# First pair's score operands padded with zeros, its first shift after four blocks, and every queue's order chosen with a backward pass

## The chip, the cores and the metric

One core of one Trainium2 chip runs the whole program. The metric is the device time of one execution in microseconds (us); of several runs the median counts. Five queues work side by side: TensorE (PE, matmuls, with PEld for its weight loads), VectorE (DVE), ScalarE (ACT), GpSimd (POOL) and SyncE (SP), which issues every DMA here. The operands lie in a memory of 128 partitions (SBUF); matmuls write into the banks of PSUM.

## The reference, cut to what matters

Attention with averaged query pairs is followed by a gated unit. For 8 batches and 8 heads, keys 1152 x 64 and 576 averaged queries:

```python
q_pool = q.reshape(B, H, S // 2, 2, D).mean(axis=3)        # 576 x 64
scores = q_pool @ k.T / sqrt(D)                            # 576 x 1152
scores = scores - scores.max(-1)
attn = exp(scores); attn = attn / (attn.sum(-1) + 1e-9)
x = attn @ v                                               # heads side by side: 8 x 576 x 512
h = relu(x @ w_in); u, v = h[..., :512], h[..., 512:]
v_n = (v - mean(v)) / sqrt(var(v) + 1e-6)
out = (u * (w_spatial @ v_n + b_spatial)) @ w_out
```

Everything is float32 outside. Inside, a number is split into a float16 head and a float16 rest, so that a product takes two or three float16 matmuls.

## The kernel before, in words

The 64 heads are worked in 32 pairs of two heads, four pairs to a batch. Each pair goes through these generators:

- `prep(i)` loads q and k, adds the two queries of each average (POOL), squares and sums q and k (ACT), makes power-of-two scales from that (one small matmul, then three DVE operations), and splits q and k: heads by ACT (`head`), rests by DVE (`rest`) or, from pair 8 on and in pairs 0 and 1, by POOL (`tensor_sub`). In pairs 2 to 7 (`i < EARLY`) DVE makes the rests of k. Each head has 64 rows, so a pair's two heads lie in the lower and upper 64 partitions; DMAs copy rows into operands of 128 rows (`khi`, `qhi`: k's head twice, q's head and rest below each other) and of 66 rows (`klo`, `xq`: k's rest against q's head, plus two rows that carry the shift).
- `maxima(i)` makes 27 matmuls of 128 queries by 384 keys (9 blocks t, 3 key parts n), each followed by a maximum on DVE (L751). Blocks 0 to 3 belong to the first head, block 4 holds the tails of both heads, blocks 5 to 8 belong to the second.
- `shift` turns the maxima of some blocks into two float16 rows (DVE L764 to L769, a PE transposition L773, DVE L775) and DMAs them into rows 64 and 65 of `xq` (L778). Before, the first shift covers blocks 0 to 4, the second 5 to 8.
- `attention(i)` makes 18 main score tiles (two matmuls each, L950 and L951), an exponential of each on ACT (L956), for most a split into head and rest on POOL (L976), and the products with v (PE L846 to L864), plus four tail tiles (L963, L967, ACT L972).
- From pair 8 on, `gated_unit` works on two finished batches in between: L1036 and L1103 (w_in), L1147 (spatial), L1190 (w_out). The weights arrive as float64 and are made float32 by DVE and ACT in `from_double` on tiles of 128 x 1024; `in_weights` is stepped through from pair 0 on.

The order on each queue is not the order of this program text. The class `Order` records all instructions, gives each a cost, and `pin` plays them forward on a model: of the instructions that are ready on a queue it takes the one that stands first in the text, and then ties each instruction to the one before it on its queue. `SLACK` delays a successor on another engine, `in_turn` keeps ACT's first instructions in text order.

In pairs 0 and 1 (`DIRECT`) the maxima of the first head read `xq` and `kn` in place, on 64 rows; those of the second head need the DMA copies `qhi` and `khi`.

## Time and profile before

| what | before |
|---|---|
| median of 3 runs | 1167.14 us (1166.41, 1167.14, 1171.51) |
| the profiled execution's own time | 1172.69 us |
| its span, first to last instruction | 1170.9 us |
| PE busy | 1139.1 us (97%) |
| DVE, ACT, POOL busy | 858.7, 891.6, 846.5 us |
| first maximum's matmul starts | 10.72 us |
| first exponential of scores starts | 27.35 us |
| first gated-unit matmul (L1036) starts | 256.31 us |
| mean granted TensorE clock | 0.992 |

The profiled execution was 5.55 us slower than the median run, and 1.79 us of its time lie outside its span. How to read it: PE is the engine with the least idle time, so time is lost where PE is idle or its granted clock is low. A busy PE is not always a PE at its peak, since ends of matmuls are modelled; the spacing of matmul starts is the better measure. Idle time of the other engines costs nothing by itself.

### The profile page before, as it was taken

To read this page: it belongs to the slowest core of one execution; us is meant where nothing else is said; L and a number is where in the kernel's file an instruction comes from. 1 tells how busy PE (TensorE), PEld (TensorE's weight loads), DVE (VectorE), ACT (ScalarE), POOL (GpSimd) and SP (SyncE) were. 2 spreads that over 40 slices of the span, in tenths; PEclk is the share of its full clock that TensorE was granted. 3 is DMA by queue.
4 is the path that set the end of the run, shared out by engine and by line. 5 is a ranking of instruction groups with operands and counts; after the bars stand their busy time and mean duration, and the time that the engine had idled before them with its cause. 6 is when DMAs were issued, how large, how long until landed. Compare 5 with 4: busy or idle time off the path is not lost.

```text
span 1170.9 us, 33542 instructions
## 1 busy us (share of the span) xinstructions
PE 1139.1 (97%) x13297; PEld 723.9 (62%) x13297; DVE 858.7 (73%) x2240; ACT 891.6 (76%) x1697; POOL 846.5 (72%) x732
## 2 busy tenths in 40 slices
PE   4999999999999999999999999999999999999998
PEld 1567777776566666666666666666666666665453
DVE  5699999867899878766678668866668777832644
ACT  6698789988787978788777977978777877754423
POOL 3566566778887988889787978898788877883000
PEclk9799999999999999999999999999999999999999
DMA  6575456444432443565323454265433431121002
GB/s 217 153 210 147 111 164 205 139 118 139 125 107 73 122 144 103 140 180 143 90 71 85 139 133 122 69 168 163 115 104 82 127 88 20 38 65 37 1 1 81
DMA packets 88990, 132.97 MB, mean 114 GB/s; under 512 B 39872, under 2 KB 48064, under 8 KB 88832
## 3 DMA queue, kind: packets, MB, share of 16 engines
q1 hardware_dynamic: 88832, 130.82, 39.8%
q8 instruction: 104, 1.70, 0.6%
q14 instruction: 54, 0.44, 0.1%
HBM read 81.20 MB, written 9.44 MB: 77 GB/s over the span
## 4 chain that ended last, share of the span: by engine, by line
PE 82%; DVE 7%; DMA 4%; ACT 3%; POOL 1%; issue 1%; SPq 1%; DVEq 0%; ACTq 0%; POOLq 0%
PE pss L950 9%; PE pss L951 9%; PE pm L745 8%; PE pw L1190 7%; PE pw L1147 7%; PE pw L1103 6%; PE pw L1036 6%; PE o L853 5%; PE o L864 5%; PE o L859 5%; DVE mt L751 3%; PE o L846 2%; PE pss L1036 1%; PE pss L1147 1%; DMA kt<-in_kT_dram 1%; PE pss L1190 1%
## 5 line engine op out<-in xcount | busy, mean ns | idle before, releaser
L976 POOL TENSOR_TENSOR pt<-pt 128x512 f16<-128x512 f32 x528 | 580.9, 1115 | 173.2 <-ACT pt L956 167.8
L956 ACT ACTIVATE pt<-pss,esc 128x512 f32<-128x512 f32 x576 | 389.2, 690 | 115.4 <-PE pss L951 107.9
L751 DVE TENSOR_REDUCE mt<-pm 128x1 f32<-128x384 f32 x733 | 387.5, 549 | 106.3 <-PE pm L745 90.6
L950 PE MATMUL pss<-qhi,khi 128*128 128x512 f16 x576 | 220.6, 383 | 3.9 <-ACT ptl L972 2.1
L951 PE MATMUL pss<-xq,klo 66*128 66x512 f16 x576 | 221.1, 384 | 0.0
L745 PE MATMUL pm<-khi,qhi 128*128 128x384 f16 x643 | 198.1, 326 | 5.2 <-DMA khi<-kn 3.4
L853 PEld LDWEIGHTS <-pt 128*128 128x128 bf16 x2112 | 125.1, 99 | 68.4 <-issue 3.0
L853 PE MATMUL o<-vp,pt 128*128 128x65 f16 x2112 | 157.3, 193 | 1.5 <-DVE xm L872 1.5
L864 PE MATMUL o<-vp,pt 128*128 128x65 f16 x2112 | 154.7, 193 | 0.0
L859 PE MATMUL o<-vp,pt 128*128 128x64 f16 x2112 | 153.1, 193 | 1.1 <-DVE vp L405 1.1
L864 PEld LDWEIGHTS <-pt 128*128 128x128 f16 x2112 | 113.7, 98 | 36.6 <-issue 1.8
L859 PEld LDWEIGHTS <-pt 128*128 128x128 bf16 x2112 | 101.8, 98 | 3.8 <-issue 1.2
L745 PEld LDWEIGHTS <-qhi 128*128 128x128 f16 x744 | 71.1, 99 | 45.6 <-issue 7.1
L1036 PE MATMUL pw<-wi_h,xg 128*128 128x512 f16 x240 | 89.2, 378 | 0.0
L1103 PE MATMUL pw<-xg,wi_h 128*128 128x512 f16 (+1 forms) x336 | 82.6, 325 | 0.0
L751 DVE TENSOR_REDUCE mt<-pw 128x1 f32<-128x384 f32 x131 | 70.4, 546 | 16.5 <-PE pw L745 11.6
L976 POOL TENSOR_TENSOR ptl<-ptl 128x1152 f16<-128x1152 f32 x32 | 69.9, 2184 | 17.4 <-ACT ptl L972 17.4
L972 ACT ACTIVATE ptl<-pss,esc 128x256 f32<-128x256 f32 (+1 forms) x128 | 64.1, 500 | 23.7 <-PE pss L967 23.7
L1147 PE MATMUL pw<-ws_h,vv 128*128 128x512 f16 x216 | 79.2, 379 | 0.0
L1190 PE MATMUL pw<-wo_h,vv 128*128 128x512 f16 x216 | 78.5, 378 | 0.0
L951 PEld LDWEIGHTS <-klo 66*128 66x128 f16 x576 | 56.4, 98 | 31.1 <-issue 8.6
L950 PEld LDWEIGHTS <-khi 128*128 128x128 f16 x576 | 56.5, 98 | 21.3 <-issue 4.3
(255 smaller groups left out, 2503.8 us busy)
## 6 DMA issues: line engine op xcount, KB each, us to landing
vt<-in_v_dram SPq DMA_DIRECT2D x56, 576.0 KB
qt<-in_qT_dram SPq DMA_DIRECT2D x32, 576.0 KB
kt<-in_kT_dram SPq DMA_DIRECT2D x32, 576.0 KB
khi<-kn SPq DMA_DIRECT2D x128, 144.0 KB
out_dram<-row SPq DMA_DIRECT2D x24, 256.0 KB
qhi<-xq SPq DMA_DIRECT2D x64, 72.0 KB
klo<-klo SPq DMA_DIRECT2D x32, 144.0 KB
u<-in_w_in_dram SPq DMA_DIRECT2D x3, 1024.0 KB
```

The lines of the kernel that those rows point to most:

```text
L745: nc.tensor.matmul(pm[:, :W], lhsT=q[:, c0 : c0 + P], rhs=k[:, n * NB : (n + 1) * NB, :], start=True, stop=True,)
L751: nc.vector.reduce_max(out=mt[:, t, n : n + 1], in_=pm[:, :W], axis=AX.X)
L853: nc.tensor.matmul(o[:, t], lhsT=top[:, cols], rhs=vp[:, D : D + D1], start=c == 0 and t == 0, stop=False, skip_group_check=True,)
L859: nc.tensor.matmul(o[:, t, 0:D], lhsT=top[:, cols], rhs=vp[:, 0:D], start=False, stop=False, skip_group_check=True)
L864: nc.tensor.matmul(o[:, t], lhsT=rst[:, cols], rhs=vp[:, D : D + D1], start=False, stop=c == NC - 1, skip_group_check=True,)
L950: nc.tensor.matmul(o, lhsT=khh[:, h, c, :], rhs=qhl[:, h, q], start=True, stop=False)
L951: nc.tensor.matmul(o, lhsT=KL[0:KR, h, c, :], rhs=X[0:KR, h, q], start=False, stop=True)
L956: nc.scalar.activation(pt, ps, AF.Exp, bias=0.0, scale=esc)
L976: nc.gpsimd.tensor_sub(t.bitcast(F16)[..., 0::2], t, t.bitcast(BF16)[..., 1::2])
L1036: nc.tensor.matmul(ph, lhsT=rows(xa, cc, c0, c0 + P), rhs=wa[:, cc, DH:DF], start=n == 0, stop=n == 3 * NCC - 1,)
L1147: nc.tensor.matmul(pv, lhsT=l, rhs=r[:, 0:MAIN], **fl)
L1190: nc.tensor.matmul(py, lhsT=ga[:, fc, c0 : c0 + P], rhs=wa[:, fc, :], start=m == 0, stop=m == end - 1)
```

## The change

- **First pair's operands.** For pair 0, q's heads go into `xz`, a tile of 128 rows per head whose other 64 rows are zero; the maxima of both heads multiply it with `kn`, which holds both heads' keys, so no row copy comes before them. The score products of pair 0 run on all 128 rows of `klo` and `xq` (rows 66 to 127 zero), and the copy of the two constant rows (L678 before) is gone for pair 0. New memsets on DVE zero these rows. The first half of k's head is made by DVE, not ACT.
- **First shift.** In pair 0 it covers blocks 0 to 3 (`cut = 4`), and pair 0's tail tiles come after main tiles 5 to 8 rather than 1 to 4.
- **Smaller moves.** `lnp` is made by POOL, not DVE. For batch 0 the squares of v take one ACT instruction of 1152 columns per pair, not two of 576. In pairs 4 to 7 the rests of k move from DVE to POOL, with one more ACT pass over k. `in_weights` is stepped from pair 4 on (`W_PAIR`), at rate 0.4 instead of 0.14.
- **Order.** `SLACK` has new values. `pin` runs twice: a forward pass, a backward pass over the same model (which gives each instruction the latest time at which it may start), and a second forward pass that takes, of the ready instructions, the most urgent. The forward pass also models a slower TensorE clock after idle windows. `in_turn` keeps DVE's first instructions in text order as well.

```diff
-    SLACK = {("Pool", "PE"): 1400, ("Activation", "PE"): 300, ("DVE", "PE"): 400, ("SP", "PE"): 1000}
+    SLACK = {("Pool", "PE"): 724, ("Activation", "PE"): 435, ("DVE", "PE"): 444, ("SP", "PE"): 1510, ("PE", "DVE"): 50}
+    WINDOW, COLD, WARM = 3413.3, 0.34, 0.765
+    PASSES = 2
...
-                    n = min(n for n in ns if at[n] <= t)
+                    n = min((n for n in ns if at[n] <= t), key=rank.__getitem__)
...
+            if e == "PE":
+                columns, weight = g.stream[n]
+                u = t
+                while True:
+                    while u >= until:
+                        share, work = work / self.WINDOW, 0.0
+                        rate = (2.4 if share > self.WARM else 1.2) if rate < 2 else (1.2 if share < self.COLD else 2.4)
+                        until += self.WINDOW
...
+    def backward(self, g, begin, own):
...
+                    t = max(free[e], min(due[n] - own[n] for n in ns))
+                    if best is None or t < best[0]:
+                        n = max((n for n in ns if due[n] - own[n] <= t), key=begin.__getitem__)
...
+        rank = range(len(prog))
+        for k in range(self.PASSES):
+            if k:
+                rank = self.backward(g, begin, own)
+            turns, begin, own, span = self.forward(g, rank)
...
-    for t in klo:
+    for t in klo[1:]:
         nc.gpsimd.memset(t[D:KR, 1], -MROW)
+    nc.vector.memset(klo[0][D:P], 0.0)
+    nc.vector.memset(klo[0][D:KR], -MROW)
+    nc.vector.memset(xq[0][D:P], 0.0)
+    for h in range(2):
+        nc.vector.memset(qhi[NSET - 1][(1 - h) * D : (2 - h) * D, h], 0.0)
...
+        if i == 0:
+            xz, kl = qhi[NSET - 1], khi[NSET - 1][:, 0]
+            kn = ld.tile([P, NC, P], F16, name="kn")
+            nc.vector.tensor_scalar_mul(kn[:, 0:5], k0[:, 0:5], s_k)
+            head(xz[lower, 0], q0[lower], s_q[lower])
+            head(kn[:, 5:NC], k0[:, 5:NC], s_k)
+            head(xz[upper, 1], q0[upper], s_q[upper])
...
+            for a, z in ((0, 5), (5, NC)):
+                nc.scalar.activation(k0[:, a:z], k0[:, a:z], AF.Copy, bias=0.0, scale=s_k)
+                nc.gpsimd.tensor_sub(kl[:, a:z], k0[:, a:z], kn[:, a:z])
+            nc.sync.dma_start(out=KL[lower, 0], in_=kl[lower])
+            factors(st, s, r)
+            load_kq(1)
+            yield
+            rest(qhl[lower, 1], q0[lower], s_q[lower], xz[lower, 0])
+            rest(qhl[upper, 1], q0[upper], s_q[upper], xz[upper, 1])
+            nc.sync.dma_start(out=qhl[upper, 0], in_=qhl[lower, 1])
...
-            if i < EARLY:
+            if i < 4:
                 head(kn[:, a:z], k0[:, a:z], s_k)
                 yield
                 rest(KL[:, 0, a:z], k0[:, a:z], s_k, kn[:, a:z])
...
-                    if i < DIRECT and h == 0:
+                    if i == 0:
+                        q, k = st["xz"][:, h], st["kn"]
+                    elif i == 1 and h == 0:
...
-            if t == 4:
-                yield from shift(st, mt, pm, 0, 5)
+            if t == cut - 1:
+                yield from shift(st, mt, pm, 0, cut)
...
+        rows = P if i == 0 else KR
...
-            Pace(weights, W_RATE, W_AT if i == 0 else 0),
+            Pace(weights if i >= W_PAIR else None, W_RATE),
```

On PE, pair 0, behind the twelve maxima of blocks 0 to 3 (`xq`, `qhi` and `qd` hold q, `kn`, `khi` and `klo` hold k). Before:

```order
L745 MATMUL pm<-kn,xq_113 128x384
...
L950 MATMUL pss<-qhi_119,khi_116 128x512
...
L732 MATMUL pw<-kn,qd_122 128x384
...
L773 MATMUL pw<-ident_h,wide_133 128x128
...
L745 MATMUL pm<-khi_116,qhi_119 128x384
...
L951 MATMUL pss<-xq_113,klo_107 128x512
```

and now:

```order
L861 MATMUL pm<-kn,qhi_123 128x384
...
L846 MATMUL pw<-kn,qd_124 128x384
...
L889 MATMUL pm<-ident_h,wide_137 128x128
...
L861 MATMUL pw<-kn,qhi_123 128x384
...
L1068 MATMUL pss<-qhi_121,khi_118 128x512
L1069 LDWEIGHTS klo_107
L1069 MATMUL pss<-xq_114,klo_107 128x512
```

The transposition of the first shift (L773, now L889) no longer stands behind all three tail maxima, the second head's maxima read `kn` and not the copy `khi`, and between the transposition and the first complete score product stand the third tail maximum and ten maxima of the second head, where nine of the second head stood before.

On SP, the DMAs of pair 0 from the load of pair 1's keys on. Before:

```order
L546 DMA kt<-in_kT_dram 128x1152
L673 DMA klo_107<-klo_107 64x1152
L674 DMA qhi_119<-xq_113 64x576
L675 DMA xq_113<-xq_113 64x576
L676 DMA khi_116<-kn 64x1152
L677 DMA khi_116<-kn 64x1152
L678 DMA klo_107<-klo_107 2x1152
L778 DMA xq_113<-mr 1x5x128 x2
```

and now:

```order
L629 DMA kt<-in_kT_dram 128x1152
L894 DMA xq_114<-mr 1x4x128 x2
L767 DMA qhi_121<-qhi_121 64x576
L769 DMA xq_114<-qhi_123 64x576
L770 DMA qhi_121<-qhi_123 64x576
L771 DMA khi_118<-kn 64x1152
```

The shift rows (`mr`) now go out right behind the load, ahead of the second head's copies.

On DVE, the second shift of the second pair, with a step of the weights' conversion (`vv`, 128 x 1024). Before:

```order
L764 TENSOR_REDUCE pw<-mt 128x4
L751 TENSOR_REDUCE mt<-pw 128x1
L765 TENSOR_SCALAR pw<-pw,lnp 128x4
L432 SCALAR_TENSOR_TENSOR vv<-vv 128x1024
L768 CAST wide_134<-pw 128x4
L751 TENSOR_REDUCE mt<-pm 128x1
L769 TENSOR_TENSOR wide_134<-pw,wide_134 128x4
```

and now:

```order
L880 TENSOR_REDUCE pw<-mt 128x4
L942 RECIPROCAL den<-den 128x4
L881 TENSOR_SCALAR pw<-pw,lnp 128x4
L941 TENSOR_SCALAR dent<-pm 128x1
...
L884 CAST wide_138<-pw 128x4
L867 TENSOR_REDUCE mt<-pm 128x1
L1044 TENSOR_SCALAR xt<-pm,dent 64x64 x2
L885 TENSOR_TENSOR wide_138<-pw,wide_138 128x4
```

The conversion of the weights has left this place: its first step on DVE now comes among the maxima of the third pair. Small operations of the values (`den`, `dent`, `xt`) stand there instead.

More of the change, by code (lines that the diff above doesn't have):

```diff
@@ L3 @@
 from contextlib import ExitStack
+from types import SimpleNamespace
 import concourse.bass as bass
@@ L165, in cost @@
         if lane == "SP":
-            if "DMA" not in ins.opcode:
+            if "DMA" not in ins.opcode and "Dma" not in ins.opcode:
                 return 0, 2400
@@ new lines, in streamed, with forward @@
+    def streamed(self, ins):
+        x = ins.ins[0].bass_ap
+        wide = x.dtype == F32
+        return math.prod([d[1] for d in x.ap][1:]) * (4 if wide else 1), x.ap[0][1] / 128 * (0.5 if wide else 1)
+    def forward(self, g, rank):
+        lane, cost, shared = g.lane, g.cost, g.shared
+        size = len(lane)
+        left = [len(pre) + len(beg) for pre, beg in zip(g.before, g.begun)]
+        ready = {e: [n for n in range(size) if lane[n] == e and not left[n]] for e in self.LANES}
+        due, there, begin, own = ([0.0] * size for _ in range(4))
+        free = dict.fromkeys(self.LANES, 0.0)
+        held, dve, wire = (0.0, 0.0), 0.0, 0.0
+        until, work, rate = self.WINDOW, 0.0, 1.2
+        turns = []
+        for _ in range(size):
@@ L263, in pin @@
                 dve = t + out - 139
+            if e == "PE":
[6 more added lines that the diff above has]
+                        until += self.WINDOW
+                    z = u + columns / rate
+                    if z <= until:
+                        work += (z - u) * weight
+                        break
+                    columns -= (until - u) * rate
+                    work += (until - u) * weight
+                    u = until
+                out += max(0, z - t - long)
+                long = max(long, z - t)
             if e == "SP":
-                wire = max(wire, t + own) + 0.58 * (out - 2400)
+                wire = max(wire, t + long) + 0.58 * (out - 2400)
                 end = wire + 1700 + 0.42 * (out - 2400)
@@ L268, in pin @@
                 end = t + out
-            free[e] = t + own
-            if e in last:
-                tc.add_manual_dep(prog[n], last[e], dep, reason="order")
-            last[e] = prog[n].name
-            for m, through in after[n]:
+            begin[n], own[n] = t, long
+            free[e] = t + long
+            for m, through in g.after[n]:
                 left[m] -= 1
@@ L284, in pin @@
                     ready[lane[m]].append(m)
-        self.span = max(free.values())
+        return turns, begin, own, max(free.values())
+    def backward(self, g, begin, own):
+        lane, cost = g.lane, g.cost
+        size = len(lane)
+        left = [len(after) for after in g.after]
+        ready = {e: [n for n in range(size) if lane[n] == e and not left[n]] for e in self.LANES}
+        due, done = [0.0] * size, [0.0] * size
+        free = dict.fromkeys(self.LANES, 0.0)
+        for _ in range(size):
+            best = None
+            for e, ns in ready.items():
+                if ns:
+                    t = max(free[e], min(due[n] - own[n] for n in ns))
+                    if best is None or t < best[0]:
+                        n = max((n for n in ns if due[n] - own[n] <= t), key=begin.__getitem__)
+                        best = (t, e, n)
+            _, e, n = best
+            ready[e].remove(n)
+            done[n] = free[e] = max(free[e] + own[n], due[n])
+            for pre, through in ((g.before[n], True), (g.begun[n], False)):
+                for m in pre:
+                    x = done[n]
+                    if through and lane[m] != e:
+                        x += cost[m][1] + self.DELAY.get((lane[m], e), 52)
+                    elif through and e != "PE":
+                        x += cost[m][1] + 34
+                    due[m] = max(due[m], x)
+                    left[m] -= 1
+                    if not left[m]:
+                        ready[lane[m]].append(m)
+        return [-t for t in done]
@@ L723, in maxima @@
         mt = sm.tile([P, NT, 3], F32, name="mt", bufs=2)
+        cut = 5 if i else 4
         for t in range(NT):
@@ L1259, in attn_sgu_kernel @@
         next(n)
-    drain(prep(0))
-    order.in_turn(tc)
+    load_kq(1, True)
+    ready = prep(0)
+    for _ in range(5):
+        next(ready)
+    order.in_turn(tc, "Activation")
     first = maxima(0)
-    for _ in range(18):
+    for _ in range(13):
         next(first)
+    order.in_turn(tc, "DVE")
+    for _ in range(2):
+        next(first)
+    drain(ready)
     for n in norms:
```

195 lines of the change are left out of this document (108 added, 87 removed).

## The prediction

> **What bounds the kernel now.** I read the page's busy times first, then the busy times by stretch, then the timeline of the first 70 us and the groups of DVE. The page says that PE has little idle time, and its row of the granted clock that the second of forty slices is slow:
>
> ```profile
> PE 1139.1 (97%) x13297; PEld 723.9 (62%) x13297; DVE 858.7 (73%) x2240; ACT 891.6 (76%) x1697; POOL 846.5 (72%) x732
> PEclk9799999999999999999999999999999999999999
> ```
>
> The stretches say where the rest goes (columns: stretch, its length, then busy time of PE, PEld, DVE, ACT and POOL, granted clock, DMA share, GB/s):
>
> ```profile
> 0.00:20.00 20.00, 7.40 (x23) 2.34 (x23) 11.81 (x30) 13.22 (x28) 10.40 (x20) 1.00 0.80 265
> 20.00:40.00 20.00, 15.09 (x107) 7.07 (x107) 13.71 (x35) 15.06 (x29) 9.96 (x9) 0.84 0.39 87
> 34.00:51.00 17.00, 17.00 (x81) 7.45 (x81) 8.73 (x17) 8.10 (x14) 9.85 (x9) 0.51 0.76 203
> 51.00:61.00 10.00, 10.00 (x146) 8.36 (x145) 7.62 (x23) 9.60 (x20) 4.72 (x5) 1.00 0.31 108
> 60.00:256.00 196.00, 188.13 (x2364) 140.34 (x2363) 178.73 (x457) 171.56 (x333) 132.28 (x107) 1.00 0.55 158
> 256.00:420.00 164.00, 161.41 (x1938) 101.20 (x1937) 140.44 (x352) 141.24 (x278) 140.84 (x117) 1.00 0.43 120
> 420.00:1060.00 640.00, 639.88 (x7997) 407.01 (x7995) 451.28 (x1218) 495.79 (x932) 537.14 (x468) 1.00 0.39 107
> ```
>
> From 420 to 1060 us PE is idle for 0.12 us in 640: nothing is to be had there, and what is won earlier stays won, because PE then does the same matmuls at the same pace. PE is idle for 12.6 us in the first 20 and for 4.9 in the next 20. From 34 to 51 it is never idle, but at a granted clock of 0.51. From 60 to 256 (pairs 1 to 7) it is idle for 7.9 us, with DVE busy for 91% and ACT for 88%: three engines close to full. From 256 to 420 it is idle for 2.6 us.
>
> The start in detail:
>
> ```profile
> 9.00 0.15 DVE L389 TENSOR_SCALAR qks<-pm 128x2 int32<-128x2 int32 x1
> 9.18 0.77 ACT L402 ACTIVATE xq<-qt,qks 128x576 f16<-128x576 f32 x1 [0.71 <-DVE qks L389]
> 10.72 0.48 PE L745 MATMUL pw<-kn,xq 64*128 64x384 f16 x1 [2.04 <-ACT kn L402]
> 13.43 0.55 DVE L751 TENSOR_REDUCE mt<-pw 128x1 f32<-128x384 f32 x1
> 13.89 0.55 DVE L751 TENSOR_REDUCE mt<-pm 128x1 f32<-128x384 f32 x1
> 19.07 0.18 DVE L764 TENSOR_REDUCE pw<-mt 128x5 f32<-128x15 f32 x1
> 20.37 0.28 DVE L775 CAST mr<-pw 10x128 f16<-10x128 f32 x1 [0.39 <-PE pm L378]
> 22.86 1.51 SPq L778 DMA_DIRECT2D xq<-mr  x2
> 23.75 0.48 PE L745 MATMUL pm<-khi,qhi 128*128 128x384 f16 x1 [3.42 <-DMA khi<-kn]
> 26.93 0.60 PE L951 MATMUL pss<-xq,klo 66*128 66x512 f16 x2
> 27.35 1.26 ACT L956 ACTIVATE pt<-pss,esc 128x512 f32<-128x512 f32 x2 [1.07 <-PE pss L951]
> ```
>
> DVE's maxima come every 0.46 us and set the pace from 11 to 19. Then PE waits 3.42 us for a row copy of k, and the shift rows, ready at 20.65 (20.37 + 0.28), leave only at 22.86, because SP waits for another copy, the constant rows of `klo`:
>
> ```profile
> SPq L678 <- DMA klo<-klo: 3.2, 1, 3.2
> ```
>
> **Term A, the first pair's start: -2.3 us.** Until the scales (9.15) nothing changes: ACT's squares set that time. The new memsets on DVE are of 1152, 576, 2304 and twice 288 columns; by 1.07 us for 1152 columns on POOL (3.21 for three, below) they take 4.3 us, from about 1 to 5.3, and the slow copies behind them (2.10 in the row below, and a cast of at most that) end between 7.4 and 9.5. The scales are done at 9.15 now, so they cost 0 to 0.5 us; I take 0.
>
> ```profile
> 1.94 3.21 POOL L355 MEMSET klo<- 2x1152 f16 x3
> 2.06 2.10 DVE L342 COPY ident<-ident 64x64 f32<-64x64 f32 x2
> ```
>
> DVE now makes the first half of k's head beside ACT's 0.77 us for q, so the first maximum can start at about 10.1 (10.72 before). Twelve maxima at 0.46 (5.5) with 0.7 more to begin and end come to 16.3, where fifteen came to 19.07. From the shift's first operation to the end of `mr` it took 1.58 us (19.07 to 20.65); a rest of q (0.8, row L405 below) now stands ahead of `mr` on DVE. So `mr` is done at about 18.7, and SP sends it at once: 1.5 us for its two DMAs and half of that for the rest of q give 20.9 before the last operand is on its way. When it lands I can only bound: at once, or after the 5.60 us that the chain of waits gives for the copy of k issued at 18.02.
>
> ```profile
> 18.02 5.60 DMA khi<-kn
> 30.72 1.41 DVE L405 SCALAR_TENSOR_TENSOR vp<-xg,vs,vp 128x576 f16<-128x576 f32 x1
> 32.25 0.80 DVE L405 SCALAR_TENSOR_TENSOR qhi<-qt,qks,xq 128x576 f16<-128x576 f32 x1
> ```
>
> That puts the first score product between 20.9 and 26.5. PE's own order (one tail maximum and ten of the second head, each behind DVE at 0.46, from 18.7 on) gives 23.8. With two products at the slow clock, 0.43 each, the first exponential starts at 24.7 to 27.4; I take 25.0 against 27.35, because in the new order SP has sent everything but the shift rows and that rest of q by the time `mr` is done. Behind a late product stand all further maxima and values on PE. Bounds: 0 to -3.
>
> **Term B, the half clock: -6 us.** Spacing of matmuls shows the clock: 512 columns take 0.22 us at 28 us and 0.43 us at 49 us.
>
> ```profile
> 28.29 0.38 PE L950 MATMUL pss<-qhi,khi 128*128 128x512 f16 x1
> 28.51 0.38 PE L951 MATMUL pss<-xq,klo 66*128 66x512 f16 x1
> 49.05 0.63 PE L951 MATMUL pss<-xq,klo 66*128 66x512 f16 x1
> 49.48 0.63 PE L950 MATMUL pss<-qhi,khi 128*128 128x512 f16 x1
> 32.18 0.28 PE L859 MATMUL o<-vp,pt 128*128 128x64 f16 x4 [1.09 <-DVE vp L405]
> ```
>
> The clock fell at 34 us, after a stretch in which PE stood behind DVE (the 1.41 us above, then a wait of 1.09). Seventeen us at 0.51 are work for 8.7, so 8.3 us are lost where nothing else binds; afterwards ACT is full (9.60 of 10), so part of them would be lost anyway. In the new order pair 0's six first exponentials and their score products come ahead of pair 1's heads on ACT, and pair 0's products use 128 rows rather than 66, so PE has work in store when the stall came before; I take 6 of 8.3. Bounds: 0 (the clock falls again) to -8.3.
>
> [...]
>
> **Term C, work taken off DVE in pairs 1 to 7: -4 us.** The rests of k that DVE makes are these twelve, for pairs 2 to 7:
>
> ```profile
> L405 DVE SCALAR_TENSOR_TENSOR klo<-kt,qks,kn 128x640 f16<-128x640 f32 (+1 forms) x12 | 10.5, 874 | 0.0
> 14.82 0.14 DVE L667 TENSOR_SCALAR lnp<-lnp 128x1 f32<-128x1 f32 x1
> ```
>
> Eight of twelve move, 7.0 us, and `lnp` adds some 1 us (seven of 0.14). POOL takes them: it was busy for 132 of 196 us, and eight subtractions of 1.3 us (row below) fit. ACT gets a second pass over k, eight of about 0.75 us by its row of 640 columns, 6 us on top of 171.6 of 196; so ACT becomes as full as DVE and I count half of the 8. Bounds: 0 to -8. If POOL's cover were gone, the exponentials' splits behind the subtractions would be late by up to 2.6 us once a pair.
>
> ```profile
> L402 ACT ACTIVATE kn<-kt,qks 128x640 f16<-128x640 f32 (+1 forms) x10 | 7.7, 768 | 0.0
> L705 POOL TENSOR_TENSOR klo<-kt,kn 128x640 f16<-128x640 f32 (+1 forms) x44 | 56.6, 1287 | 0.2 <-ACT kn L704 0.2
> ```
>
> **Term D, the order by urgency: -4 us.** Before, a step of the weights' conversion, which nobody needs before 256 us, can stand in the middle of a shift, for which the next pair's scores wait:
>
> ```profile
> 66.86 0.22 DVE L765 TENSOR_SCALAR pw<-pw,lnp 128x4 f32<-128x4 f32 x1
> 66.98 1.22 DVE L432 SCALAR_TENSOR_TENSOR vv<-vv 128x1024 int32<-128x1024 int32 x1
> 68.12 0.16 DVE L768 CAST wide<-pw 128x4 f16<-128x4 f32 x1
> 256.31 0.38 PE L1036 MATMUL pw<-wi_h,xg 128*128 128x512 f16 x1
> ```
>
> At most PE's 7.9 us of idle time between 60 and 256 come back; I take half. Upwards: conversion steps crowd into pairs 4 to 7, where four more of them (1.2 each) than before would cost up to 4.8. Bounds: +4.8 to -7.9.
>
> **Term E, from 256 us to the end: 0.** The same matmuls, 2.6 us of idle time up to 420 and the fixed last 111 us. Bounds: +4 to -2.6.
>
> **Sum.** -2.3 - 6 - 4 - 4 = -16.3 us, against the profiled execution's own 1172.69 (span 1170.9 and 1.79 around it): 1156.4, say **1156 us**. The median of the runs shown is 1167.14, so that this is -11 us, or -1.0%, there; the profiled execution was 5.55 us above it, and I suppose, without a trace of the other runs, that its slow stage was longer than theirs. That is a reason not to go lower.
>
> **Rivals.**
>
> *The clock falls again.* If any stall of a few us follows the first warm stretch, for instance while ACT makes pair 1's heads, PE works at half speed until it has caught up. For it: the trace shows such a fall after a stretch that was only partly idle. Against it: the fuller rows and the work in store. Term B goes: 1156 + 6 = 1162. [...]
>
> *ACT and DVE are full anyway.* Between 60 and 256 us they have 179 and 172 us of 196, and only 7 leave DVE while 6 come to ACT. If their sum, not the order, sets the pace, terms C and D vanish: 1156 + 8 = 1164.
>
> *Slower: the tighter order starves PE later.* The whole program is reordered, with half the slack between POOL and PE. POOL, whose splits PE needs, is the fullest of the feeders from 420 on (537 of 640 us).
>
> ```profile
> L976 POOL TENSOR_TENSOR pt<-pt 128x512 f16<-128x512 f32 x431 | 470.6, 1107 | 105.7 <-ACT pt L956 101.2 <-DMA qd<-xq 1.7 <-DMA qhi<-xq 1.2
> ```
>
> If each of these 431 splits came late by 0.05 us on a PE that is never idle, 21.6 us would be lost, the gain and 5 more: 1156 + 21.6 = 1178 against 1172.69, about 1172 by the median. It decides from 0.04 us a split on (16.3 / 431). Against it: POOL itself waits for ACT before its splits (101.2 us in all), so it isn't late.
>
> **How the numbers follow.** The forecast gets 0.66, the clock 0.16, full engines 0.10, starvation 0.08. The low bound adds the rest of A (0.7), B (2.3), C (4) and D (3.9), not all at once: 1145. The high one is the second rival and a us: 1165; above it lie starvation and, with little, B, C and D failing together. Within the forecast I give 1150 to 1162. What a measurement of this kernel can tell from no change is 0.5%, 5.8 us: faster means under 1161.3, slower over 1173.0. Faster: 0.66 x 0.97 and half of the first rival and a third of the second, 0.75; same: 0.17; slower: 0.08, all from starvation.
>
> **What would show it.** A: the first exponential at 24.7 to 26.5 us and no wait of PE for a copy of k before it. B: no stretch of several us at a clock near 0.5 once it is full, and the first gated matmul at 238 to 246 us rather than 256.31 (A to D together). C and D: DVE below 91% busy from 60 us to that matmul, PE idle there for under 5 us. E: PE idle for about 0 from 420 us on. The forecast is wrong if the granted clock falls again, if pairs 1 to 7 still take 196 us, or if PE waits for POOL later.

## The result and the profile after

The changed kernel is slower: 1178.6 us median of 5 executions (1177.73 to 1180.62), against 1167.14 (1165.96 to 1172.36) for the kernel before on the same chip, a ratio of 1.0088 with a 95% interval of 1.0058 to 1.0117. The forecast was 1156, with 1145 to 1165. The profiled execution of the changed kernel took 1177.73 us, with a span of 1175.9. Ratios here and below leave out two executions that are far longer than all others, one of 3003.81 us of the kernel before and one of 1945.04 us of a later version (conversion from pair 1).

Busy times and granted clock on the page of the changed kernel:

```profile
PE 1136.2 (97%) x13297; PEld 723.4 (62%) x13297; DVE 869.3 (74%) x2207; ACT 896.3 (76%) x1697; POOL 870.6 (74%) x771
PEclk8999999999999999999999999999999999999999
```

Its busy times by stretch (stretch, length, then PE, PEld, DVE, ACT, POOL, granted clock, DMA share, GB/s):

```profile
20.00:60.00 40.00, 36.90 (x398) 23.84 (x398) 35.20 (x87) 32.78 (x62) 25.70 (x22) 0.95 0.64 171
60.00:256.00 196.00, 184.68 (x2263) 136.57 (x2262) 170.95 (x421) 171.92 (x332) 145.88 (x120) 0.98 0.53 155
256.00:420.00 164.00, 160.96 (x1960) 101.64 (x1959) 140.12 (x347) 141.41 (x280) 139.72 (x120) 1.00 0.42 114
420.00:1060.00 640.00, 634.32 (x7895) 402.64 (x7892) 455.64 (x1190) 492.83 (x923) 540.21 (x482) 1.00 0.40 107
```

From 60 to 256 us DVE has 8 us less to do than before (170.95 for 178.73), as meant, but PE is idle for 11.32 us there, not for less than 7.87. From 420 to 1060, where PE was idle for 0.12 us, it is now idle for 5.68.

Three moments date the loss. The first is the first exponential of scores; the second the transposition of pair 0's output (L1014 after, L898 before), which I take as the end of pair 0; the third the first gated matmul (L1155 after, L1036 before). Each row gives how often in the window asked for, durations, and first and last start. After:

```profile
L1074 ACT ACTIVATE pt<-pss,esc x2: 687/687/687, 24.1 to 24.7; 128x512 f32<-128x512 f32 x2
L1014 PE MATMUL pm<-ident,xm x4: 272/272/273, 59.4 to 59.8; 128*128 128x128 f32 x4
L1155 PE MATMUL pw<-wi_h,xg x1: 377/377/377, 253.6 to 253.6; 128*128 128x512 f16 x1
```

The kernel before, in the execution that the prediction read:

```profile
L898 PE MATMUL pm<-ident,xm x4: 273/273/329, 69.9 to 70.3; 128*128 128x128 f32 x4
```

Against that execution pair 0 ends 10.5 us earlier, the first gated matmul comes 2.7 us earlier (256.31 there), and the span is 5.0 us longer. So the start gained, pairs 1 to 7 gave back 7.8, and what follows the first gated matmul lost another 7.7.

Most of what pairs 1 to 7 stand behind begins in ACT's waits. ACT takes its instructions in the order that the planner tied them in. A square of k or v (L482) that stands in that order before its load has landed holds up the exponentials behind it. The groups of waits of ACT from 20 to 256 us, for loads, are these after the change (total us, times, longest):

```profile
ACT klo L482 <- DMA kt<-in_kT_dram: 11.7, 8, 2.6
ACT vt L482 <- DMA vt<-in_v_dram: 2.8, 1, 2.8
ACT vp L485 <- DMA vt<-in_v_dram: 1.1, 1, 1.1
```

PE's two largest groups of waits from 60 to 256 us stand behind ACT, directly or by way of DVE (`xg` is a pair's finished output: ACT makes its head, then DVE its rest):

```profile
PE pss L1081 <- ACT pt L1074: 4.0, 3, 2.0
PE pm L861 <- DVE xg L936: 3.2, 2, 2.2
```

PE has seven waits of 0.4 us or more in that stretch. Six of them end 2 to 4 us behind a wait of ACT for a load: 2.21, 0.65, 0.99, 2.01, 0.66 and 1.73 us, together 8.25 of PE's 11.32 us of idle time. Three in the timeline (start, length, engine, line; in brackets the engine's idle time before it and what ended that): ACT waits for a load of v until 62.59, so `xg` comes late and PE stands for 2.21 us; ACT waits for a load of k until 140.31, then works through four squares, and PE, which needs the next exponential, stands for 2.01 us; the third is like the second.

```profile
62.59 0.68 ACT L482 ACTIVATE vt<-vt 128x576 f32<-128x576 f32 x1 [2.81 <-DMA vt<-in_v_dram]
65.30 0.34 PE L861 MATMUL pm<-khi,qhi 128*128 128x384 f16 x1 [2.21 <-DVE xg L936]
140.31 1.17 ACT L482 ACTIVATE klo<-kt 128x1152 f16<-128x1152 f32 x1 [2.65 <-DMA kt<-in_kT_dram]
143.47 0.67 ACT L1074 ACTIVATE pt<-pss,esc 128x512 f32<-128x512 f32 x1
144.18 0.31 PE L1081 MATMUL pss<-qhi,khi 128*128 128x64 f16 x5 [2.01 <-ACT pt L1074]
224.53 1.16 ACT L482 ACTIVATE klo<-kt 128x1152 f16<-128x1152 f32 x1 [1.98 <-DMA kt<-in_kT_dram]
227.08 0.31 PE L1081 MATMUL pss<-qhi,khi 128*128 128x64 f16 x5 [1.73 <-ACT pt L1074]
```

From 420 us on, PE's own waits are of another kind, and before the change the same view had no row at all:

```profile
PE pm L889 <- DVE wide L885: 3.1, 2, 1.6
PE o L980 <- POOL pt L1094: 1.9, 4, 0.7
PE o L969 <- ACT pt L1074: 0.4, 2, 0.2
```

The first is a shift's transposition behind DVE, where a step that nobody waits for yet (the 1.00 us copy `te` at 633.97, first read by PE at 667.3) runs ahead of the shift:

```profile
633.97 1.00 DVE L1203 COPY te<-vv 64x512 f16<-64x512 f16 x1
635.92 0.16 DVE L885 TENSOR_TENSOR wide<-pm,wide 128x4 f16<-128x4 f32 x1
636.14 0.23 PE L889 MATMUL pm<-ident_h,wide 128*128 128x128 f16 x1 [1.46 <-DVE wide L885]
```

### The profile page after: what moved, and what is told of

It reads as the page before. It is cut to its first block, busy times and chain, and to the rows that moved or that the text cites. A ratio compares the mean times of both kernels' runs of the same rounds, so it can differ in the third digit from the quotient of the medians.

```text
span 1175.9 us, 33543 instructions
## 1 busy us (share of the span) xinstructions
PE 1136.2 (97%) x13297; PEld 723.4 (62%) x13297; DVE 869.3 (74%) x2207; ACT 896.3 (76%) x1697; POOL 870.6 (74%) x771
## 4 chain that ended last, share of the span: by engine, by line
PE 74%; DVE 5%; DMA 4%; ACT 4%; POOL 3%; issue 3%; SPq 1%; ACTq 0%; POOLq 0%; DVEq 0%
PE pss L1068 8%; PE pss L1069 8%; PE pm L861 7%; PE pw L1266 6%; PE pw L1222 6%; PE pw L1155 5%; PE pw L1309 5%; PE o L969 4%; PE o L980 4%; PE o L975 4%; DMA kt<-in_kT_dram 2%; DVE mt L867 2%; POOL pt L1094 2%; PE o L962 2%; ACT pt L1074 2%
## 5 line engine op out<-in xcount | busy, mean ns | idle before, releaser
L1069 PE MATMUL pss<-xq,klo 66*128 66x512 f16 (+1 forms) x576 | 219.9, 382 | 0.9 <-DMA khi<-kn 0.9
L861 PE MATMUL pm<-khi,qhi 128*128 128x384 f16 x637 | 194.1, 325 | 4.9 <-DVE xg L936 3.6
L980 PEld LDWEIGHTS <-pt 128*128 128x128 f16 x2112 | 110.6, 98 | 27.9 <-POOL pt L1094 3.2
L1155 PE MATMUL pw<-wi_h,xg 128*128 128x512 f16 x240 | 88.9, 378 | 0.0
L867 DVE TENSOR_REDUCE mt<-pw 128x1 f32<-128x384 f32 x131 | 69.9, 546 | 11.5 <-PE pw L861 8.9
L818 POOL TENSOR_TENSOR klo<-kt,kn 128x640 f16<-128x640 f32 (+1 forms) x56 | 75.9, 1358 | 2.3 <-ACT kn L817 2.2
L1069 PEld LDWEIGHTS <-klo 66*128 66x128 f16 (+1 forms) x576 | 56.4, 98 | 31.1 <-issue 6.7
```

Source lines behind the costliest of these rows:

```text
L861: nc.tensor.matmul(pm[:, :W], lhsT=q[:, c0 : c0 + P], rhs=k[:, n * NB : (n + 1) * NB, :], start=True, stop=True,)
L867: nc.vector.reduce_max(out=mt[:, t, n : n + 1], in_=pm[:, :W], axis=AX.X)
L980: nc.tensor.matmul(o[:, t], lhsT=rst[:, cols], rhs=vp[:, D : D + D1], start=False, stop=c == NC - 1, skip_group_check=True,)
L1069: nc.tensor.matmul(o, lhsT=KL[0:rows, h, c, :], rhs=X[0:rows, h, q], start=False, stop=True)
L1155: nc.tensor.matmul(ph, lhsT=rows(xa, cc, c0, c0 + P), rhs=wa[:, cc, DH:DF], start=n == 0, stop=n == 3 * NCC - 1,)
```

## The experiments

Where the expectations number theories: T1 lays the loss on the order by urgency (the second, backward-ranked pass), which lets ACT stand in front of late loads; T2 on the new slacks; T3 on the work that the change moved within the program. The changed planner also counts other costs for some instructions (copies and short operations on DVE above all), which the section on the change doesn't name. "Old planner" below means SLACK, one pass, instruction costs and no clock model, as in the kernel before. All of these kernels compute the whole result.

### The kernel before, profiled again

No edit. 

> The kernel before once more, unchanged, for a second profiled execution. The prediction priced the second slow-clock stage (33.7 to 50.8 us, granted clock 0.51) at 6 us from one profiled execution of 1172.69 us, 5.5 us above the median. If that stage belongs to every execution, this one has a slow stage of 14 to 21 us between 20 and 60 us and its first pair ends at 68 to 71 us. If it is an accident of the profiled execution, the stage is under 8 us or missing, the first pair ends at 62 to 66 us, and the execution takes 1166 to 1169 us.

1167.55 us (ratio 0.9995, 0.9979 to 1.001). Its profiled execution took 1165.52 us, with a span of 1163.7. The stretches of this second execution, and its end of pair 0 and first gated matmul:

```profile
20.00:60.00 40.00, 33.32 (x345) 21.42 (x346) 33.49 (x81) 31.77 (x61) 21.16 (x17) 0.99 0.59 158
59.00:62.40 3.40, 3.40 (x32) 2.20 (x31) 2.57 (x5) 3.33 (x7) 0.39 (x1) 0.50 0.82 223
60.00:256.00 196.00, 189.53 (x2363) 140.97 (x2361) 176.02 (x449) 173.17 (x335) 134.91 (x110) 0.99 0.54 160
256.00:420.00 164.00, 162.69 (x1971) 102.37 (x1970) 141.73 (x360) 139.68 (x276) 141.25 (x118) 1.00 0.44 122
420.00:1060.00 640.00, 639.88 (x7978) 406.10 (x7977) 445.61 (x1203) 494.93 (x928) 535.76 (x466) 1.00 0.39 105
```

```profile
L898 PE MATMUL pm<-ident,xm x4: 270/272/272, 64.9 to 65.3; 128*128 128x128 f32 x4
L1036 PE MATMUL pw<-wi_h,xg x2: 377/378/378, 250.4 to 250.8; 128*128 128x512 f16 x2
ACT vt L399 <- DMA vt<-in_v_dram: 4.2, 2, 3.5
ACT klo L399 <- DMA kt<-in_kT_dram: 3.7, 5, 2.1
```

The 17 us at half clock are not there; one stage of 3.4 us is. Pair 0 ends at 64.9, not 69.9. Of the 41 executions of this kernel in this comparison, 28 had a mean granted clock of 0.998 or more, with a median of 1167.2 us, and only six were below 0.996, at 1169.85 to 1171.91 us. The execution from which the prediction was made (0.992, 1172.69) was of the latter kind. So the slow stage of 17 us was an accident of that execution, as far as one more profile and the mean clocks can say.

Against this execution, the changed kernel's pair 0 ends 5.5 us earlier (59.4 for 64.9), pairs 1 to 7 up to the first gated matmul take 8.7 us more (194.2 for 185.5), and the rest 9.0 us more (922.3 for 913.3): together the 12.2 us between the spans. Of the 9.0, PE's idle time accounts for 1.7 between 256 and 420 and 5.6 from 420 on.

### One pass instead of two

```diff
-    PASSES = 2
+    PASSES = 1
```

> The changed kernel with one forward pass, ranked by text order, and all the rest of the change kept (new slack, first pair, moved work). Theory 1, the backward rank puts work that waits for DMAs ahead of the exponentials on ACT: the lead that the new start gives (10 us by the end of pair 0) is kept, ACT waits for loads of k and v between 60 and 256 us for under 5 us rather than 13, 1158 to 1167 us. Theory 2, the small slack starves PE: the slack stays, so 1174 to 1180. Theory 3, the work moved into pairs 4 to 7 fills ACT: 1174 to 1180 as well.

1185.19 us, ratio 1.0129 (1.0089 to 1.0168). Without the order by urgency it is not better, so urgency by itself isn't the cause. ACT still waits for loads of k and v for 12.5 us between 20 and 256 us (15.6 in the changed kernel).

### The slacks of before

```diff
-    SLACK = {("Pool", "PE"): 724, ("Activation", "PE"): 435, ("DVE", "PE"): 444, ("SP", "PE"): 1510, ("PE", "DVE"): 50}
+    SLACK = {("Pool", "PE"): 1400, ("Activation", "PE"): 300, ("DVE", "PE"): 400, ("SP", "PE"): 1000}
```

> The changed kernel with the slack values of before, both passes kept. Theory 2 (slack): from 420 to 1060 us PE loses about 6 us and not 12.7, and the time falls to 1165 to 1172 us. Theory 1 (rank): 1175 to 1180, ACT's waits for loads as long as now. Theory 3 (moved work): 1175 to 1180.

1186.13 us, ratio 1.016 (1.0119 to 1.0202). The new slacks aren't the cause by themselves either; with the old ones, PE's idle time from 420 to 1050 us is 11.1 us.

### The program of before with the changed planner

```diff
-class Order:            # of before
+class Order:            # of the change: slacks, costs, clock model, two passes
-    order.in_turn(tc)
+    order.in_turn(tc, "Activation")
```

> The kernel before with the changed planner alone (both passes, new slack, clock model), no change of the first pair and no moved work. Theories 1 and 2: slower than before by the 8 to 15 us that the change loses after pair 0: 1174 to 1184 us. Theory 3: no loss, 1160 to 1169.

1194.71 us, ratio 1.0216 (1.0183 to 1.025): more than the whole change loses, with nothing of the program moved. From 420 us on:

```profile
420.00:1060.00 640.00, 634.58 (x7877) 402.32 (x7876) 465.49 (x1240) 498.53 (x943) 540.67 (x465) 1.00 0.41 108
```

PE is idle for 5.42 us there, for 5.68 with the whole change, and for 0.12 before. So what is lost from 420 us on needs no moved work; the changed planner alone makes as much of it. Its loss elsewhere is partly the clock, which falls four times in its profiled execution:

```profile
35.80:42.60 6.80, 6.80 (x49) 3.37 (x47) 5.29 (x12) 2.32 (x4) 4.02 (x4) 0.51 0.71 165
73.30:83.60 10.30, 7.74 (x32) 4.51 (x32) 3.81 (x11) 7.88 (x15) 4.11 (x3) 0.51 0.15 50
209.80:216.60 6.80, 6.80 (x52) 4.95 (x51) 3.92 (x11) 3.48 (x7) 2.43 (x3) 0.52 0.54 178
271.30:274.70 3.40, 3.40 (x23) 1.73 (x22) 1.91 (x6) 2.09 (x6) 3.11 (x4) 0.52 0.89 329
```

PE is busy for 24.7 us in these, so half speed costs 12.4 us there at most, for 1.7 at most in the second execution of the kernel before. Its span is 30.6 us longer than that one's (1194.3 for 1163.7): PE's idle time up to 1050 us accounts for 15.9 and the clock for up to 10.7.

### A slack for loads

```diff
-    SLACK = {("Pool", "PE"): 724, ("Activation", "PE"): 435, ("DVE", "PE"): 444, ("SP", "PE"): 1510, ("PE", "DVE"): 50}
+    SLACK = {("Pool", "PE"): 724, ("Activation", "PE"): 435, ("DVE", "PE"): 444, ("SP", "PE"): 1510, ("PE", "DVE"): 50, ("SP", "Activation"): 2500}
```

The planner then counts what ACT takes from a load or copy as ready 2.5 us later, and lets other ACT work go ahead.

> The changed kernel, with one more slack in the planner: ACT work that reads a loaded tile counts as ready 2.5 us after the modelled landing. Theory 1: ACT's waits for loads of k and v between 60 and 256 us fall from 13 to under 5 us and the time by 4 to 9 us, to 1169 to 1175. Theories 2 and 3: 1176 to 1180.

1171.06 us, ratio 1.0032 (1.0011 to 1.0054): 7.5 us less than the changed kernel. ACT's waits for loads between 20 and 256 us fall from 15.6 us to 3.1, and from 60 to 256 PE is idle for 8.88 us instead of 11.32. That is only part of the gain: the first gated matmul comes 0.7 us earlier (252.9 for 253.6), and PE's idle time falls by another 2.5 us from 256 to 420 (0.58 for 3.04) and 3.3 from 420 on (2.36 for 5.68), where most of what PE waited for in the changed kernel was not ACT. So the new order as a whole gains, and how much of the 7.5 us the late loads are worth is not shown here.

### The changed program with the old planner

```diff
-    SLACK = {("Pool", "PE"): 724, ...
+    SLACK = {("Pool", "PE"): 1400, ("Activation", "PE"): 300, ("DVE", "PE"): 400, ("SP", "PE"): 1000}
-    PASSES = 2
+    PASSES = 1
...
-            if e == "PE":
+            if False:
                 columns, weight = g.stream[n]
```

together with the instruction costs of before. 

> The changed program with the whole planner of before (its slack, costs, one pass in text order, no clock model); with these the kernel before comes out instruction for instruction. If the program's changes (first pair, first shift, moved work) are good and the planner alone loses, pair 0 ends by 62 us, the lead of 8 to 10 us lasts and the time is 1155 to 1163 us. If the work moved into pairs 4 to 7 does harm, 1170 to 1180.

1177.66 us, ratio 1.0081 (1.0054 to 1.0108). The whole planner put back changes nothing that can be told from the changed kernel (1.0088). PE's idle time from 420 to 1050 falls to 2.2 us, and that from 60 to 256 rises to 13.3: ACT waits for loads for 12.0 us here too.

### Without the clock model

```diff
-            if e == "PE":
+            if False:
                 columns, weight = g.stream[n]
```

> The changed kernel without the planner's model of a slower clock. Theory: a modelled slow start makes the planner believe that loads have more time than they have; then ACT's waits for loads of k and v (16 us between 20 and 256) fall under 8 and the time to 1165 to 1172 us. Rival, the clock model has no part in it: 1175 to 1185.

1187.8 us, ratio 1.0161 (1.0116 to 1.0207). No gain from that part alone.

### Controls: numbers moved that should not matter

The changed kernel, and the kernel before twice:

```diff
-("DVE", "PE"): 444      # changed kernel
+("DVE", "PE"): 440
-("DVE", "PE"): 400      # before, first control
+("DVE", "PE"): 396
-("Pool", "PE"): 1400    # before, second control
+("Pool", "PE"): 1390
```

> The changed kernel with one slack (DVE to PE) of 440 rather than 444 ns, a control: the order changes in some hundreds of places and nothing in its rules. If the loss belongs to the rules: 1176 to 1181 us. If the planner's outcome scatters with any small change: outside that by 4 us or more, and single runs of the planner's parts say little.

> The kernel before with one number of its planner moved by 4 ns (the slack from DVE to PE, 396 for 400), which changes the order of a few hundred instructions and nothing else. If any order by such a rule is as good as another, and the loss of the changed kernel comes from its own steps, the ratio lies between 0.997 and 1.003. If the order of the kernel before is a favourable one among its neighbours, the ratio lies between 1.003 and 1.012.

> The kernel before with its planner's slack from POOL to PE at 1390 for 1400, which changes the order of several thousand instructions on PE and nothing else. Same two readings as for the 4 ns: 0.997 to 1.003 if orders of this kind are equal, 1.003 to 1.015 if the order of the kernel before is a favourable one.

The changed kernel moved by 4 ns takes 1176.6 us (ratio 1.0084, 1.0051 to 1.0118). The two of before take 1168.02 (1.0003, 0.9984 to 1.0022) and 1171.59 (1.0033, 1.0017 to 1.0049). So a planner number by itself is worth up to 4 us, through nothing but another order, and differences of 2 to 4 us between the kernels here carry no verdict on a cause. The order of before is a good one, but one of its two neighbours is as good.

### Old planner and the slack for loads

The changed program with the old planner and, in SLACK, `("SP", "Activation"): 2500`. 

> The changed program with the planner of before plus the 2.5 us of slack for ACT work that reads a loaded tile. Theory (ACT behind late loads costs whatever the planner): 2 to 5 us faster than the same without that slack, 1152 to 1160. Rival (with the planner of before ACT waited for loads only 5 us, so nothing is to be had): the same within 3 us.

1168.94 us, ratio 1.0008 (0.9997 to 1.002), 8.7 us less than without that slack (1177.66). In ACT's waits between 20 and 256 us no row for a load is left. Here the gain lies where the waits were: the first gated matmul comes at 249.7 us for 256.4, and PE is idle from 60 to 256 us for 7.17 us instead of 13.28:

```profile
60.00:256.00 196.00, 188.83 (x2352) 140.03 (x2350) 177.68 (x431) 177.84 (x341) 150.72 (x122) 1.00 0.54 156
```

The level of before, to within the measurement: with the other planner too, letting ACT pass by loads that are late takes the larger part of the loss away.

### Before with the slack for loads

```diff
-("SP", "PE"): 1000}
+("SP", "PE"): 1000, ("SP", "Activation"): 2500}
```

> The kernel before with the late-load slack alone. There ACT waited for loads 6 us between 60 and 256 and 6 from 256 to 1060; a gain of 0 to 4 us, 1163 to 1168. If the slack is worth 8 us here too, 1158 to 1161, then it is no cure of the change but a gain of its own, and the comparison of the changed program with the kernel before needs the slack on both sides.

1175.67 us, ratio 1.0072 (1.0057 to 1.0087). Here too ACT no longer waits for loads, and still the kernel is 8.5 us slower, with 10.2 us of PE's idle time from 60 to 256. So the slack isn't good as such. It pays in the changed program, where ACT waited for loads for 12.0 to 15.6 us, and not in the program of before, where it waited for 5.2 and 7.9 in two executions. Against the second execution of the kernel before, PE is idle for 3.7 us more from 60 to 256 and 2.7 more from 256 to 420, and its mean granted clock from 60 to 142 us is 0.92, for 0.99 there. Why this order empties PE stays open.

### The moved work put back, in parts

On the kernel with the old planner and the slack for loads, first the rests of k of pairs 4 to 7 go back to DVE, then the weights' conversion goes back to all pairs, then both:

```diff
-            if i < 4:
+            if i < EARLY:
                 head(kn[:, a:z], k0[:, a:z], s_k)
...
-    W_RATE = 0.4
-    W_PAIR = 4
+    W_RATE = 0.14
+    W_PAIR = 0
```

> As the last, with only the rests of k on DVE again (the conversion still from pair 4 on). If the extra pass over k on ACT and the later release of the single tile of k are the cost: 1161 to 1165 us. If the conversion's place is the cost: 1167 to 1172.

> As the last but one, with only the conversion stepped from pair 0 on again (the rests of k still on POOL). If the conversion's place is the cost: 1161 to 1165 us; if the rests are: 1167 to 1172.

> The planner of before with the late-load slack, the changed first pair, but the rests of k in pairs 4 to 7 on DVE again and the weights' conversion stepped from pair 0 on as before. Theory 3 (the moved work costs what the new start wins): pairs 4 to 7 take 104 us as in the kernel before, not 110, and the time is 1158 to 1164 us, faster than the kernel before. Rival (the moved work is harmless, some other part of the change loses): 1167 to 1171, as with the moves.

| rests of pairs 4 to 7 | conversion | median, us | ratio |
|---|---|---|---|
| POOL | from pair 4 | 1168.94 | 1.0008 (0.9997 to 1.002) |
| DVE | from pair 4 | 1170.44 | 1.0022 (1.0008 to 1.0035) |
| POOL | from pair 0 | 1167.65 | 0.9999 (0.9986 to 1.0013) |
| DVE | from pair 0 | 1166.36 | 0.9988 (0.9976 to 1.0001) |

Moving the rests is worth -1.5 us in one row pair and +1.3 in the other: nothing. The later conversion costs 1.3 and 4.1 us, within what the controls show for another order. What it buys shows earlier: with the conversion back in pair 0 the first exponential still starts at 24.7 us (last row of the table) or 24.8, but pair 0 ends no earlier than in the kernel before (64.5 and 64.9 us, for 64.9), where the two versions with the conversion from pair 4 on end it at 61.6 and 62.6. In the version of the last row:

```profile
L1012 PE MATMUL pm<-ident,xm x4: 272/273/306, 64.5 to 64.8; 128*128 128x128 f32 x4
```

### A neighbour of the best, and the conversion from pair 1 or 2

```diff
-("DVE", "PE"): 400      # neighbour
+("DVE", "PE"): 396
-    W_PAIR = 0          # the other two
+    W_PAIR = 1          # rate 0.16; then 2, rate 0.2
```

> The changed kernel's first pair with the complete planner of before, the slack of 2500 from SP to ACT, the rests of pairs 4 to 7 and the weights' conversion back where they were, and the slack from DVE to PE at 396 for 400 (without the last number: 1166.36 us, ratio 0.9988). If waiting for loads is what spreads the time from order to order, this neighbour stays within 0.996 to 1.003. If 1166.36 was a favourable order too, it lies between 1.003 and 1.012.

> The changed kernel's first pair, the complete planner of before, the slack of 2500 from SP to ACT and the rests of pairs 4 to 7 back on DVE, with the weights' conversion from pair 1 on at a rate of 0.16 (from pair 0 at 0.14: 1166.36 us, the first pair ending at 64.5 us). If the conversion in pair 0 is what takes the start's gain back, the first pair ends at 61 to 62.5 us, pairs 1 to 7 still take 186 to 188 us, and the median is 1162 to 1165 us. If the later pairs have no room for it, pair 7 ends at 251 to 254 us as before and the median is 1166 to 1170 us.

> The same with the conversion from pair 2 on at a rate of 0.2. First pair 61 to 62.5 us and pair 1 by 88 to 91 us in either case. 1162 to 1165 us if the pairs behind have room, 1166 to 1171 us if they have not, with the loss in pairs 2 to 7.

1167.73 us (0.9999, 0.9984 to 1.0014), 1166.39 (0.9985, 0.997 to 1.0001) and 1169.85 (1.0014, 0.9998 to 1.0031). None beats the kernel before by what can be measured. With the conversion from pair 1 on, the first pair does end earlier, at 62.2 for 64.9, and the gain is gone by the first gated matmul (249.8 for 250.4):

```profile
L1012 PE MATMUL pm<-ident,xm x4: 272/273/278, 62.2 to 62.6; 128*128 128x128 f32 x4
L1153 PE MATMUL pw<-wi_h,xg x2: 379/380/380, 249.8 to 250.3; 128*128 128x512 f16 x2
60.00:142.00 82.00, 79.47 (x997) 58.72 (x995) 80.65 (x198) 73.35 (x140) 57.26 (x47) 1.00 0.57 163
```

DVE is busy for 80.65 of 82 us from 60 to 142: behind the first pair it has no room left. That is where the second rival of the prediction looked ("ACT and DVE are full anyway"). It isn't the whole answer, since from 142 to 200 us DVE has 3.5 us to spare here (54.54 of 58) and PE still falls behind; why is open.

## Why the prediction was wrong

**Term B and the base cancel.** The -6 us for the stage at half clock were read off one execution, 5.5 us above the median, and the second profile and the granted clocks of the 41 executions say that a typical one has no such stage. The forecast suspected as much, but only as a reason not to go lower. Since base and term carry the same accident, the number 1156 hardly depends on it: against the median, the -11 us are A, C and D (-10.3) and nothing for B. What was wrong is the sense that B was a gain that could be had, and with it the first rival's price. That fuller rows keep the clock up, an argument of the prediction against a new fall, no run tests.

**Term A, right for the first exponential, and not kept.** It starts at 24.1 (forecast 25.0, between 24.7 and 27.4; 27.35 in the execution read then and 28.0 in the second), a little beyond the bound of -3. Pair 0 ends 5.5 us before that of the second execution, but that end isn't term A's alone: with the conversion back in pair 0, the start's 3.3 us (24.7 for 28.0) are gone by the end of pair 0 (64.5 for 64.9). That all further work of the pair follows an earlier start was assumed, and these two versions don't bear it out.

**The clock falls again, and little of the loss is that.** The prediction named a new fall as a sign against it. The granted clock shows three: 6.8 us at 16.9, where DVE's maxima set the pace (6.73 of 6.80), and twice 3.4 us later, where each can cost 1.7 at most:

```profile
16.90:23.70 6.80, 6.12 (x17) 1.69 (x18) 6.73 (x20) 5.59 (x12) 0.20 (x1) 0.50 0.37 114
68.10:71.50 3.40, 3.39 (x17) 1.66 (x18) 2.80 (x6) 3.03 (x7) 3.40 (x3) 0.50 0.99 345
228.50:231.90 3.40, 3.40 (x24) 2.70 (x22) 1.71 (x3) 3.40 (x9) 1.68 (x2) 0.50 0.47 161
```

The first is no loss against the kernel before. There the granted clock is given as 1.00 from the start, but the spacing of matmuls says otherwise: products of 384 columns start 0.32 us apart at 24.35 and 0.17 us apart at 27.51, so PE had not yet reached full speed.

```profile
24.35 0.52 PE L745 MATMUL pm<-khi,qhi 128*128 128x384 f16 x1
24.67 0.52 PE L745 MATMUL pw<-khi,qhi 128*128 128x384 f16 x1
27.51 0.33 PE L745 MATMUL pw<-khi,qhi 128*128 128x384 f16 x1
27.68 0.32 PE L745 MATMUL pm<-khi,qhi 128*128 128x384 f16 x1
```

So in this trace a granted clock of 1.00 ahead of the first recorded fall is not to be trusted, and the mean clocks of the two kernels can differ by that alone. The two later stages cost 3.4 us at most, for 1.7 at most in the second execution of the kernel before: 1.7 of the 12.2 us between the spans. Behind the first 25 us the version with the old planner and the slack for loads has no slow stage (granted clock 1.00 from 20 to 256 us) and the best version has 10.2 us of them (54.8 to 58.2 and 71.9 to 78.7 us, at 0.50), and the version without is the slower (1168.94 and 1166.36). So the first rival is not where the changed kernel's loss is. That any stall of a few us brings half speed until PE has caught up was its supposition: in the changed kernel 3.4 us with PE busy for 1.78 (from 61.3) were followed by a granted clock of 1.00, and in the execution read for the forecast the full clock came back at 51.0 us while PE had no idle time before or behind (17.00 of 17.00 us, 10.00 of 10.00).

**Term C, wrong, though its sign was met.** DVE's load from 60 to 256 fell by 7.8 us, as worked out; its share is 87%, below the 91% that was to show the step right. PE got nothing from it, since PE was not waiting for DVE's rests there but for exponentials and for `xg`, and ACT for loads. The table above puts the rests at -1.5 to +1.3 us.

**Term D, the wrong sign.** This is the step that failed first. The order by urgency was to bring back half of PE's 7.9 us of idle time between 60 and 256; it went up by 3.4 us (4.9 against the second profile). The prediction looked at what urgency does to work that nobody needs yet, and not at what stands ahead of an engine's queue when a load is late. The loads of k and v had no term and no bound, although ACT's wait for them stood in the trace of before (3.6 and 1.6 us between 60 and 256). The waits don't hang on urgency alone: between 20 and 256 us they are 12.0 us with the old planner on the changed program, 11.8 with the changed planner on the program of before, and 15.6 with both. In the changed kernel, 8.25 of PE's 11.32 us of idle time follow them. Two experiments bear on their size: the slack for loads takes off 8.7 us with the old planner, where in the profiled executions the gain lies ahead of the first gated matmul (6.7 us), and 7.5 with the changed one, where most of it lies behind that. Both are more than any control moved the time. But other changes of the planner moved the changed kernel by 7 to 9 us the other way (one pass, the old slacks, no clock model), and the same slack made the program of before 8.5 us slower, so that part of the gain may be a luckier order; no run here separates the two.

**Term E, mis-sized.** 0 with a bound of +4; measured 1.7 (256 to 420) and 5.6 us of idle time (from 420 on) against the second profile. "What is won earlier stays won, because PE then does the same matmuls at the same pace" was the failing sentence. PE's time there was full because the order fed it, and the changed planner alone, on the program of before, empties it by as much (5.4). The third rival, the tighter order that starves PE later, had the right place and the right side, at a chance of 0.08. Its mechanism is only partly the right one: 1.9 us are PE behind POOL's splits, as it said, and 3.1 are shifts behind DVE.

**What adds up and what doesn't.** In medians, the way from the changed kernel to the best version is -7.5 (the slack for loads), -2.1 (the old planner), -2.6 (the moved work back): 1178.6 to 1166.36. These medians come from several chips; by the ratios to the kernel before on each it is -6.5, -2.8 and -2.3. Only the first of the three exceeds what the controls moved. What is left in that version are the first pair's new operands, its shorter shift, the small moves of `lnp` and of v's squares, a new order of the program text at the start, and the slack for loads, and it takes as long as the kernel before (0.9988, 0.9976 to 1.0001). With the same planner and slack the program of before takes 1175.67 us on that chip, so the parts that are left can't be priced by one such pair of orders. That the changed planner is bad for the program of before by 27 us (1194.71 for 1167.7 on the same chip), and worth only 2.1 in the changed program, is measured. Of the 30.6 us by which its profiled execution is longer than the second one of the kernel before, up to 10.7 are falls of the clock and 15.9 are idle time of PE; why the order empties PE is not found, and none of the planner's parts alone shows it. A second buffer for `kt`, which might let loads start earlier, was not tried.

**Slips in the working.** The low bound of 1145 was said to take the rests of A, B, C and D "not all at once", but 0.7 + 2.3 + 4 + 3.9 is 10.9, and 1156 - 10.9 is 1145: it takes all of them. The miss was on the other side, so nothing hangs on it. By the working of term A, fifteen maxima from 10.72 would end at 18.3 and not at 19.07, so its 0.7 us to begin and end is too little; the first shift's first operation came at 16.59 rather than 16.3.

## What to carry to other kernels

Before a stage of one profiled execution is priced, compare that execution's time and granted clock with the other runs: a slow stage that lies above the median is not there to be won. ACT here worked in the order that it was given, and stood for up to 2.8 us at an instruction whose load was late, with exponentials behind it. So a planner that believes a load has landed puts the instruction that needs it ahead of work that could go on; look in the waits for "compute engine behind a load" whenever an order is planned anew, and try allowing for late loads there, on the old program too. Re-plan the old program with the new planner first, and move a number that does not matter as a control: here that alone was worth up to 4 us, and the planner alone 27.

## What the runs showed of the hardware

The stage of 17 us belonged to the execution, not to the program: the same kernel before ran 17 us at 0.51 in one execution and 3.4 us at 0.50 in the other. In the two programs of the comparison the stages are 3.4, 6.8 or 17.0 us long, that is one, two or five times 3.4; with the changed planner on the program of before there are stages of 6.8, 10.3, 6.8 and 3.4 us (its rows stand above). What went before these falls was no idle stretch: PE was busy for 1.29 of the 3.4 us before the one at 59.0 in the kernel before, and for 2.01 and 1.67 before the two later ones of the changed kernel (68.1 and 228.5):

```profile
55.60:59.00 3.40, 1.29 (x13) 0.77 (x12) 3.28 (x6) 2.75 (x7) 0.66 (x1) 1.00 0.70 154
```

```profile
61.30:64.70 3.40, 1.78 (x27) 1.11 (x23) 0.88 (x3) 1.92 (x5) 0.00 (x0) 1.00 0.96 323
64.70:68.10 3.40, 2.01 (x11) 1.22 (x11) 3.40 (x8) 2.90 (x7) 1.34 (x1) 1.00 0.89 299
225.10:228.50 3.40, 1.67 (x25) 0.94 (x24) 2.49 (x8) 3.40 (x9) 0.69 (x2) 1.00 0.58 156
```

A stretch of 1.78 just before the first was not followed by a fall, so that share alone does not decide it. The long stage lasted through full work: PE was busy for 17.00 of its 17.00 us at 0.51. The changed planner's clock model assumes a slower clock after idle windows; these rows don't show that, since PE worked for 38 to 59% of each stretch ahead of a fall. What starts a stage and what ends it, no run here shows.

The loads of k (576 KB) took 7.37 and 7.05 us where they stood in the changed kernel's chain of waits, at 84.86 and 197.17 us.
